# Gated delta rule with a gated convolution behind it: a third tap of the convolution as a diagonal product on TensorE, and a new order of all instructions

## The chip, the core and the metric

The kernel runs on one core of a Trainium2 chip. The engines are named as the profile names them: PE (TensorE, the matrix engine; PEld is its loading of weights), DVE (VectorE), ACT (ScalarE), POOL (GpSimd), and SP, which here only issues transfers (DMA). The metric is the device time of one execution in microseconds. Three runs of the kernel before took 335.29, 337.51 and 338.4 us, so its median is 337.51 us.

## The reference

Two stages follow each other. The first is a recurrent attention with the delta rule, for 4 batches and 8 heads, 768 tokens, head size 48:

```python
k_n = k / (norm(k) + 1e-6)
for t in range(S):
    y[:, :, t] = einsum('bhd,bhde->bhe', q[:, :, t], state)
    v_old      = einsum('bhde,bhd->bhe', state, kt)
    state     += bt * einsum('bhd,bhe->bhde', kt, vt - v_old)
```

The second takes the 8 heads of a token as one row x of 384 numbers, and has a causal convolution over time with 5 taps for each channel, a sigmoid gate, and two products with 384x384 matrices:

```python
gate_pre = sum(conv_w[k] * xp[:, k:k + S, :] for k in range(5))   # xp: x behind 4 rows of zeros
out = (sigmoid(gate_pre) * (x @ w_val)) @ w_out
```

All of it is in float32. The three weight arrays come to the kernel as the bits of float64 numbers, which it turns into float32 itself.

## The kernel before, in words

The 768 tokens are cut into 12 chunks of 64. Two chunks make a group, so there are 6 groups. All 32 pairs of batch and head are worked on at once; two heads share the 128 partitions, 16 such pairs lie side by side.

**Preparation of a group (`prep`).** For each half of a chunk a load brings keys and queries (`KQ`, three buffers, 448 KB each), and PE makes the products of all keys with all keys and queries (`gram`, 16 matmuls). ACT copies them out (`GL`) and gathers the diagonal blocks (`D`). DVE then inverts 32x32 triangular blocks: a transpose into `TLP`, the norms and coefficients (`coef`), rows and merges (`row`, `mergez8`, `zmul`, `tred` and so on, with some of the large products on POOL), and two transposes out, `TTR` and `TNA`. This is the longest stretch of work on DVE. PE combines the blocks with `z` and `t` (32 small matmuls each for a chunk), and ACT copies the results to `BD`.

**The chain of a chunk (`chain`).** `e` (keys on the state), `u` (the inverse on the values), `SPS` (the update of the state, kept in PSUM) and `y` (the output). Each step waits for a copy of the step before: `VT` on DVE, `US` on ACT. POOL scales the values (`vscale`) and masks the products of queries and keys (`att`, into `AQ`). The rows of `y` go to `X` by a copy on ACT and, where they change partitions, by six small transfers from `YS` for each chunk.

**The second stage of a chunk (`moe`).** For each of 3 blocks m of 128 channels: `conv`, the taps listed in `PTAPS`, as matmuls of 128x128 diagonal weights `DW` with 256 columns of `X` into a bank of PSUM; `tap`, the other taps, each one instruction on DVE that multiplies a shifted view of `X` by a column of weights and adds it to the same bank; `sig`, the sigmoid, on ACT; `val`, 3 matmuls of 256 columns; `gate` on DVE. Then two output blocks `out` of 3 matmuls with 384 columns each, copied by ACT and stored.

A float32 matmul counts as two instructions on PE in the profile, so a `conv` with two taps is x4 there, a `val` x6, an `out` x6, a `gram` x32.

**What sets the order.** Every step is recorded in a plan with a number, and the table `ORDER` lists these numbers in the order in which they are issued; each engine works through its own part of this list strictly in turn. A negative number -n in the table stands for n calls of `keep_warm`, a matmul of zeros (`SPS<-ZW`, 128x128) whose result nobody uses; it occupies PE only. Loads stand in the same table, and SP issues them in that order. A load waits in SP's queue until its buffer is free, and everything behind it waits with it.

The weights pass through two staging places in turn (`plan_weights`): a load, five steps on bits (one on ACT, four on DVE: L275, L277, L279, L282), a copy on ACT and two instructions on POOL. There are seven such passes: the taps, three for `w_val`, three for `w_out`. `tap_weights` makes `DW` out of the identity and the taps, one ACT instruction for each tap and block.

```python
PTAPS = (0, 1)                                   # taps that go to PE
for i, k in enumerate(PTAPS):                    # conv(m), L700
    PE.matmul(p, DW[:, m, i, :], x[:, m, :, k:k + C], start=(i == 0), stop=(i == len(PTAPS) - 1))
V.scalar_tensor_tensor(out=p, in0=x[:, m, :, k:k + C], scalar=CW[:, m, k:k + 1], in1=p,   # tap(m, k), L705
                       op0=ALU.mult, op1=ALU.add)
for k in (k for k in range(KS) if k not in PTAPS):
    add("DVE", 0.48, tap, (m, k), r=XT_ + [("Xh", c), "CW"], w=kp)
```

Of the kernel before, what the change touches and what calls it, by code (L numbers as in the profile page):

```python
# [26 lines left out]
PTAPS = (0, 1)  # L27
# [4 lines left out]
    -1, 8, 16, 65, 160, 9, 70, -1, 3, 1, 2, 7, 75, -1, 10, 11, 12, -1, 13, -2, 14, 17, 0, 4, 6, -1, 15, 24, 64, 18,  # L32
    19, 20, 21, 22, -8, 66, 67, -1, 23, 69, 68, -1, 71, 80, -1, 72, 106, 32, 76, -1, 73, 74, -2, 77, 163, 272, 161,
    267, 25, 85, 79, 78, -1, 26, 27, -2, 81, -4, 28, 29, 30, 31, 82, -3, 33, 83, 84, 268, -2, 86, 34, 35, 36, 269,
    -1, 37, 38, 87, 270, 39, -4, 273, 88, 89, 110, 215, 107, 48, 162, 311, 277, 282, 90, -1, 274, 91, 276, 275, 92,
    93, -1, 94, 95, 96, 97, 98, -1, 99, -1, 100, 101, 102, 103, 111, 104, -1, 278, 279, 281, 280, 49, 283, -3, 472,
    40, 105, 112, 113, 114, 115, 116, 284, -7, 117, 118, -1, 41, 119, 120, 121, 122, 123, 125, 124, 5, 126, -1, 127,
    50, -2, 128, 42, -4, 43, 129, 51, 130, 131, 132, -1, 133, -2, 134, 44, 135, -1, 136, 45, 137, 138, -1, 139, 271,
    -3, 285, 286, 46, 47, 108, 140, 287, 288, 52, 141, -50, 142, 473, 143, 474, 144, 289, 475, 146, 147, 368, 109,
    56, 477, 482, 148, 290, 291, 292, 293, 294, 295, 53, 296, 149, -1, 478, 150, 54, 55, 479, 297, 298, 57, 145,  # L40
    299, 300, 301, 302, 168, 303, 481, 169, 304, 305, 58, 306, 307, 314, 315, 59, 316, 151, 317, 60, 318, 152, 170,
    153, 319, 61, 320, 62, 321, 63, 175, 156, 171, 172, 480, 322, 173, 164, 167, 216, 176, 155, 174, 677, 487, 166,
    309, 157, 177, 158, 476, 154, 159, 323, 217, 324, 483, 484, 218, 178, 486, 488, 219, 325, 489, 485, 221, 328,
    329, 220, 330, 331, 222, 362, 513, 165, 363, 181, 184, 183, 180, 308, 182, 312, 179, 227, 310, 326, 327, 364,
    332, 490, 224, 223, 228, 369, 333, 334, 336, 370, 340, 337, 229, 230, 186, 193, 187, 188, 194, 189, 200, 231,
    233, 235, 234, 236, 232, 682, 190, 313, 335, 367, 237, 185, 195, 225, 201, 196, 202, 191, 226, 197, 338, 192,
    339, 203, 204, 198, 245, 341, 199, 205, 238, 252, 343, 246, 239, 492, -1, 491, 493, 206, 342, 211, 348, 212,
    207, -1, 344, 494, 208, 678, 345, 346, 247, 495, 240, 496, 248, 241, 497, 679, 681, 680, 498, -1, 499, -1, 500,
    -1, 683, 501, 253, 502, 684, -1, 356, 249, 503, 504, 254, 505, 506, 507, 508, 349, 686, 242, 685, 509, 510, 350,
    357, 351, 243, 255, 511, 512, 519, 520, 352, 256, 347, 521, 244, 522, 523, 250, 353, 354, 251, 524, 525, 526,  # L50
    257, 355, 358, 359, 371, 372, 258, 527, 420, 210, 213, 692, 209, 366, 687, 516, 365, 374, 528, 373, 529, 688,
    689, 380, 530, 375, 691, 360, 361, 376, 690, 381, 377, 693, 259, 573, 214, 887, 514, 533, 534, 260, 262, 261,
    531, 378, 694, 421, 535, 536, 422, 537, 382, 718, 892, 379, 695, 383, 532, 569, 389, 385, 386, 538, 423, 387,
    384, 388, 882, 424, 263, 426, 432, 539, 425, 541, 542, -1, 427, 543, 540, 391, 433, 696, 428, 429, 430, 545,
    544, 392, 393, 431, 264, 394, 515, 546, 398, 434, 395, 435, 396, 547, 574, 698, 697, 572, 390, 549, 517, 883,
    405, 550, 440, -1, 441, -1, 439, 438, 437, 436, 399, 397, 884, 548, 575, 699, -1, 457, 700, 458, 551, 553, 554,
    -1, 885, 886, 552, 562, 701, 459, 460, 555, 888, 889, 702, 406, 703, 461, 443, 407, 704, 400, 705, 890, 556,
    557, 891, 706, 444, 707, -1, 558, 559, -2, 893, 445, 708, 709, 446, 710, 711, -1, 894, 712, 401, 713, 568, 1087,
    897, 265, 266, 447, 408, 714, 715, 450, 716, 717, 451, 724, 402, 895, 896, 409, 403, 410, 576, 560, 725, 726,
    404, 727, 728, 411, 448, 563, 564, 416, 729, 452, 730, 453, 731, 449, 732, 733, 734, 412, 417, 561, 454, 565,  # L60
    566, 413, 419, 567, 418, 415, 625, 721, 414, 570, 735, 455, 462, 898, 577, 456, 518, 736, 737, 463, 578, 738,
    739, 899, 571, 1092, 579, 900, 585, 580, 586, 581, 582, 740, 468, 464, 719, 741, 742, 743, 583, 469, 465, 584,
    626, 746, 744, 587, 466, 1097, 923, 747, 627, 750, 628, 629, 588, 631, 901, 630, 748, -2, 632, 442, 745, 774,
    720, 590, 594, 637, -2, 633, 593, 778, 592, 589, 591, 722, 470, 830, 635, 634, 638, -1, 639, 749, 751, 902, 640,
    775, 646, 645, 643, 776, 773, 641, 642, 471, 644, 467, 772, 752, 753, 903, 610, 779, 595, 777, 723, 611, 780,
    904, 612, 754, 1088, 755, 756, 766, 767, 1089, 596, 603, 1102, 1091, 757, 1090, 905, 597, -1, 906, 613, -2,
    1093, 614, 1094, -1, 907, 598, 908, 909, 604, 910, 599, 911, 605, 912, 913, 606, -1, 662, 759, 760, 1096, 1095,
    914, 663, 915, 664, 916, 917, 665, 918, 600, 758, 636, 761, 763, 615, 762, 666, 607, 919, 920, 616, 648, 921,
    649, 922, 650, 929, 781, 1098, 667, 782, 930, 668, 931, 651, 932, 784, 652, 1099, 764, 783, 933, 934, 1101, 765,
    935, 785, 1103, 655, 787, 1104, 936, 937, 656, 938, 786, 831, 1100, 1105, 939, 788, 601, 602, 940, 657, 658,  # L70
    768, 769, 789, 770, 771, 659, 1106, 608, 790, 609, 832, 941, 942, -1, 653, 833, 660, 943, 834, 791, 792, 983,
    924, 654, 944, 661, 945, 946, 835, 947, 621, 836, 793, 948, 837, 617, 842, 798, 799, 1128, 797, 794, 796, 795,
    838, 618, 622, 843, 840, 844, 925, 979, 949, 800, 647, 841, 845, 801, 951, 952, 953, 955, 950, 624, 623, 851,
    927, 848, 619, 977, 620, 1035, 849, 847, 808, 802, 803, 815, 809, 804, 816, 810, 673, 811, 805, 839, 817, 954,
    818, 984, 806, 819, 674, 675, 676, 846, 978, 850, 928, 982, 956, 812, 1107, 807, 957, 820, 669, 813, 821, 985,
    958, 959, 960, 860, 867, 963, 1108, 961, 962, 670, 1109, 861, 1110, 814, 853, 964, 965, 826, 1111, 862, 868,
    869, 1112, 870, 1113, 863, 1114, 1115, 854, 966, 871, 972, 827, 872, 672, 671, 828, 1131, 829, 981, 1116, 864,
    855, 1117, 1118, 873, 1119, 1120, 856, 1121, 865, 1122, 1123, 967, 971, 857, 1124, 968, 1125, 1126, 969, 986,
# [758 lines left out]
```

## Time and profile before

| | |
|---|---|
| median of three runs | 337.51 us |
| the profiled execution, whole | 338.18 us |
| its span, first to last instruction | 336.5 us |
| PE busy with matmuls | 308.9 us (92%) |
| PE loading weights | 251.0 us (75%) |
| DVE busy | 261.8 us (78%) |
| ACT busy | 193.3 us (57%) |
| POOL busy | 124.7 us (37%) |

The profiled execution lies 0.67 us above the median, and 1.68 us of it lie outside the span. Two cautions: matmuls are pipelined and their ends are modelled, so PE's busy time also holds short gaps; and the granted clock of PE (PEclk, 1.00 is full speed) differs between stages. A row of a table by stages gives for one stretch of time the busy microseconds of each engine with the number of its instructions, then the mean granted clock, the mean busy share of the 16 DMA engines, and the GB/s that they moved. In a row of the timeline or the chain the first number is the start, the second the length, and what stands in brackets is the idle time of that engine just before and what ended it.

### The profile page before, as it was taken

How to read it: one execution, taken by the hardware profiler on the slowest of the kernel's cores; microseconds unless marked ns; L12 is line 12 of the kernel's file. 1: busy time of each engine (PE TensorE's matmuls, PEld its weight loads, DVE VectorE, ACT ScalarE, POOL GpSimd, SP SyncE). 2: the span in 40 equal slices, each digit the busy share in tenths (PEclk: the TensorE clock that was granted, in tenths of full speed). 3: DMA queues.
4: the chain of work that ended last, by engine and by line, in shares of the span. 5: the costliest groups of instructions: out<-in, count | busy, mean ns of one | idle time of the engine just before them, and what ended most of it. 6: DMA issues, size and time to landing. Idle time of an engine off the chain costs nothing.

```text
span 336.5 us, 13878 instructions
## 1 busy us (share of the span) xinstructions
PE 308.9 (92%) x6050; PEld 251.0 (75%) x6050; DVE 261.8 (78%) x565; ACT 193.3 (57%) x428; POOL 124.7 (37%) x92
## 2 busy tenths in 40 slices
PE   8936999699779979999999999999999999999994
PEld 6835899589757868777787887868776787786872
DVE  5368999999698994999997899896998779511640
ACT  6742402987636865598455897534875633575221
POOL 5441355244980005960057620485200583300000
PEclk9987599755997998999999999999999999999999
DMA  7899805045440573625087664014341742301222
GB/s 213 265 205 262 191 0 158 3 113 170 128 123 1 137 185 113 179 59 159 15 222 209 186 131 150 8 57 131 107 115 37 204 109 79 96 4 27 47 47 47
DMA packets 20283, 39.47 MB, mean 117 GB/s; under 512 B 8112, under 2 KB 11312, under 8 KB 20224
## 3 DMA queue, kind: packets, MB, share of 16 engines
q1 hardware_dynamic: 20224, 38.60, 43.5%
q8 instruction: 47, 0.77, 1.0%
q14 instruction: 12, 0.10, 0.1%
HBM read 32.69 MB, written 4.72 MB: 111 GB/s over the span
## 4 chain that ended last, share of the span: by engine, by line
PE 60%; DVE 14%; ACT 8%; DMA 7%; POOL 4%; issue 3%; SPq 3%; POOLq 0%; ACTq 0%; DVEq 0%
PE out L726 14%; PE val L715 11%; PE conv L700 7%; PE gram L358 4%; PE e L581 4%; PE u L581 3%; PE SPS L769 3%; PE y L649 3%; SPq L221 3%; PE SPS L581 2%; PE y L651 2%; PE z L458 2%; DMA AQ<-in_w_val_dram 2%; PE t L478 2%; DMA X<-YS 2%
## 5 line engine op out<-in xcount | busy, mean ns | idle before, releaser
L705 DVE SCALAR_TENSOR_TENSOR conv<-X,CW,conv 128x256 f32<-128x256 f32 x108 | 49.9, 484 | 14.2 <-PE conv L700 12.1
L715 PE MATMUL val<-X,WV 128*128 128x256 f32 x216 | 52.5, 390 | 0.0
L726 PE MATMUL out<-WO,GT 128*128 128x384 f32 x144 | 50.9, 495 | 0.0
L421 POOL TENSOR_TENSOR PR<-TLP,TT__83 128x768 f32<-128x768 f32 x5 | 10.6, 2118 | 97.0 <-DVE TT__83 L416 97.0
L715 PEld LDWEIGHTS val<-X,WV 128*128 128x128 f32 x216 | 40.3, 192 | 6.9 <-ACT GL L216 0.3
L769 PE MATMUL SPS<-ZW 128*128 128x128 f32 x294 | 43.7, 302 | 0.4 <-ACT US L643 0.4
L769 PEld LDWEIGHTS SPS<-ZW 128*128 128x128 f32 x294 | 39.4, 210 | 5.1 <-issue 3.6
L358 PE MATMUL gram<-KQ 48*64 48x128 f32 x768 | 33.4, 311 | 10.2 <-DMA KQ<-in_kq_dram 8.5
L700 PE MATMUL conv<-X,DW 128*128 128x256 f32 x144 | 37.5, 396 | 2.7 <-POOL X L695 2.3
L726 PEld LDWEIGHTS out<-WO,GT 128*128 128x128 f32 x144 | 26.2, 189 | 15.0 <-DVE GT L719 0.2
L216 ACT ACTIVATE GL<-gram 128x512 f32<-128x512 f32 x48 | 27.1, 596 | 16.7 <-PE gram L358 16.2
L358 PEld LDWEIGHTS gram<-KQ 48*64 48x64 f32 x768 | 26.1, 156 | 13.6 <-issue 9.3
L649 PE MATMUL y<-AQ,US 112*64 112x64 f32 x384 | 31.0, 237 | 4.7 <-issue 4.0
L649 PEld LDWEIGHTS y<-AQ,US 112*64 112x64 f32 x384 | 26.8, 147 | 8.9 <-issue 7.7
L700 PEld LDWEIGHTS conv<-X,DW 128*128 128x128 f32 x144 | 26.5, 194 | 8.4 <-POOL X L695 2.7
L559 POOL TENSOR_SCALAR_AFFINE_SELECT AQ<-GL 64x1024 f32<-64x1024 f32 x24 | 29.2, 1216 | 7.2 <-PE y L649 3.5
L216 ACT ACTIVATE D<-GL 32x512 f32<-32x512 f32 (+1 forms) x36 | 22.6, 628 | 15.8 <-DVE TT__83 L441 15.1
L581 PE MATMUL u<-VT,BD 64*64 64x48 f32 x768 | 30.6, 233 | 0.7 <-DVE VT L633 0.6
L581 PEld LDWEIGHTS u<-VT,BD 64*64 64x64 f32 x768 | 27.7, 148 | 3.8 <-issue 1.1
L651 PE MATMUL y<-AQ,US 128*48 128x64 f32 x384 | 29.1, 233 | 0.0
L633 DVE TENSOR_TENSOR VT<-e,VT 128x384 f32<-128x384 f32 x22 | 12.3, 557 | 20.1 <-PE e L581 14.1
L637 ACT ACTIVATE US<-u 64x384 f32<-64x384 f32 x24 | 11.6, 483 | 27.9 <-PE u L581 27.8
(97 smaller groups left out, 609.7 us busy)
## 6 DMA issues: line engine op xcount, KB each, us to landing
KQ<-in_kq_dram SPq DMA_DIRECT2D x24, 448.0 KB, 5.6
KF<-in_kf_dram SPq DMA_DIRECT2D x11, 448.0 KB, 4.6
KT<-in_kt_dram SPq DMA_DIRECT2D x12, 384.0 KB, 4.2
AQ<-in_qf_dram SPq DMA_DIRECT2D x24, 192.0 KB, 4.5
VT<-in_vt_dram SPq DMA_DIRECT2D x12, 384.0 KB, 4.0
out_dram<-OS SPq DMA_DIRECT2D x48, 96.0 KB, 2.7
AQ<-in_w_val_dram SPq DMA_DIRECT2D x3, 384.0 KB, 6.0
AQ<-in_w_out_dram SPq DMA_DIRECT2D x3, 384.0 KB, 7.6
```

The costliest lines, as they stand in the source:

```text
L216: A.activation(out=out, in_=in_, func=AF.Copy, **kw)
L358: PE.matmul(bank["g", g, c, 2 * h + s][64 * a:64 * a + 64, 128 * j:128 * (j + 1)], x[:, 0:C], x, start=True, stop=True)
L559: G.affine_select(out=AQ[c][r0:r0 + 64, j], in_=GL[r0:r0 + 64, c * NP:(c + 1) * NP, 64:128], pattern=[[0, NP], [1, C]], compare_op=ALU.is_ ...
L581: return lambda: PE.matmul(*a, stop=True, **k)
L633: V.tensor_tensor(out=v, in0=bank["e", ch, h][:, 0:HB * D].rearrange("p (u x) -> p u x", x=D), in1=v, op=ALU.add)
L649: PE.matmul(p[0:64, C * j:C * j + C], US[ch % 3][0:112, 0, h, D * j:D * j + 64], AQ[c][0:112, 0, pp, :], start=True, stop=True)
L651: PE.matmul(p[64:112, C * j:C * j + C], us[:, 1, h, j, :], AQ[c][:, 1, pp, :], start=True, stop=True)
L700: PE.matmul(p[:, 0:B * C].rearrange("p (b t) -> p b t", t=C), DW[:, m, i, :], x[:, m, :, k:k + C], start=(i == 0), stop=(i == len(PTAPS) - 1))
L705: V.scalar_tensor_tensor(out=p, in0=x[:, m, :, k:k + C], scalar=CW[:, m, k:k + 1], in1=p, op0=ALU.mult, op1=ALU.add)
L715: PE.matmul(p[:, 0:B * C].rearrange("p (b t) -> p b t", t=C), WV[:, k, 128 * m:128 * m + 128], xs[:, k], start=(k == 0), stop=(k == NKT - 1))
L726: PE.matmul(bank["o", ch, i][:, 0:DM], GT[k][:, 2 * i:2 * i + 2, :].rearrange("p b t -> p (b t)"), WO[:, k, :], start=(k == 0), stop=(k == ...
L769: PE.matmul(SPS[0][:, 384:512], ZW, ZW, start=False, stop=True, skip_group_check=True)
```

## The change

`PTAPS` becomes `(0, 1, 2)`. So each `conv` has three matmuls instead of two, `DW` holds nine diagonal blocks instead of six, and of the five taps two remain on DVE instead of three. Over 12 chunks and 3 blocks, 36 instructions leave DVE and 36 matmuls come to PE.

The numbers of the plan's steps shift with it, and the table `ORDER` is another one throughout: 1256 steps instead of 1292, and 172 calls of `keep_warm` instead of 147. Nothing else differs; line numbers are 3 lower after the table.

```diff
-PTAPS = (0, 1)
+PTAPS = (0, 1, 2)
...
 ORDER = [
-    -1, 8, 16, 65, 160, 9, 70, -1, 3, 1, 2, 7, 75, -1, 10, 11, 12, -1, 13, -2, 14, 17, 0, 4, 6, -1, 15, 24, 64, 18,
+    0, 8, 16, 160, 9, 65, 1, 10, 11, 12, 13, 70, 75, 14, 17, -1, 15, 6, 4, 64, 24, 18, 2, 19, 20, 21, -10, 66, 67,
...
```

Where the instructions stand, at three places. **First**, PE ahead of the first `z`, the first work that needs the inverse of group 0. Before (the second `gram` here is the eighth of the program):

```order
L358 MATMUL gram<-KQ_67 64x128 x16
L769 MATMUL SPS_120<-ZW 128x128 x3
L358 MATMUL gram<-KQ_68 64x128 x16
L769 MATMUL SPS_120<-ZW 128x128 x73
L458 MATMUL z<-TTR,GL_80 32x32 x32
L358 MATMUL gram<-KQ_69 64x128 x16
L478 MATMUL t_632<-ZS,TNA 32x32 x32
```

The same place now:

```order
L355 MATMUL gram<-KQ_67 64x128 x16
L766 MATMUL SPS_120<-ZW 128x128 x10
L355 MATMUL gram<-KQ_68 64x128 x16
L766 MATMUL SPS_120<-ZW 128x128 x107
L455 MATMUL z<-TTR,GL_80 32x32 x32
L766 MATMUL SPS_120<-ZW 128x128 x11
L355 MATMUL gram<-KQ_69 64x128 x16
L766 MATMUL SPS_120<-ZW 128x128 x2
L475 MATMUL t_701<-ZS,TNA 32x32 x32
```

Between the eighth `gram` and `z` stand 107 matmuls of zeros instead of 73. **Second**, SP's loads at the same time. Before (the first row is the 20th load of the program, the second brings the keys for the eighth `gram`):

```order
L221 DMA KQ_67<-in_kq_dram 112x1024
L221 DMA KQ_68<-in_kq_dram 112x1024
L221 DMA KQ_69<-in_kq_dram 112x1024
L221 DMA AQ_79<-in_w_out_dram 128x768
L221 DMA KF_76<-in_kf_dram 112x1024
L221 DMA KT_71<-in_kt_dram 128x768
L221 DMA AQ_79<-in_w_out_dram 128x768
```

Now, again from the 20th load on (here the load of `KQ_68` is the one for the eighth `gram`; `KQ_67` for the seventh was the 14th load):

```order
L218 DMA AQ_79<-in_w_out_dram 128x768
L218 DMA VT_75<-in_vt_dram 128x768
L218 DMA KT_72<-in_kt_dram 128x768
L218 DMA KQ_69<-in_kq_dram 112x1024
L218 DMA AQ_78<-in_qf_dram 48x1024
L218 DMA KQ_68<-in_kq_dram 112x1024
L218 DMA AQ_79<-in_w_out_dram 128x768
```

The keys for the eighth `gram` went from the 21st place to the 25th. Both lists of the first 25 loads hold the same things, but for one load of `KT` (384 KB) in place of one of `KF` (448 KB); the 26th is in both the last part of `w_out`. **Third**, PE around the first `z` of group 1 (`GL_81`). Before:

```order
L700 MATMUL conv<-X_98,DW 128x256 x6
L581 MATMUL SPS_121<-US_94,KT_71 48x48 x16
L715 MATMUL val<-X_98,WV 128x256 x6
L700 MATMUL conv<-X_99,DW 128x256 x2
L715 MATMUL val<-X_98,WV 128x256 x3
L700 MATMUL conv<-X_99,DW 128x256 x4
L769 MATMUL SPS_120<-ZW 128x128
L726 MATMUL out<-WO,GT_101 128x384 x6
L769 MATMUL SPS_120<-ZW 128x128
L458 MATMUL z<-TTR,GL_81 32x32 x32
L358 MATMUL gram<-KQ_67 64x128 x16
```

Now:

```order
L697 MATMUL conv<-X_98,DW 128x256 x6
L455 MATMUL z<-TTR,GL_81 32x32 x32
L697 MATMUL conv<-X_98,DW 128x256 x3
L712 MATMUL val<-X_98,WV 128x256 x3
L697 MATMUL conv<-X_99,DW 128x256 x3
L355 MATMUL gram<-KQ_67 64x128 x16
L712 MATMUL val<-X_98,WV 128x256 x3
L697 MATMUL conv<-X_99,DW 128x256 x3
L355 MATMUL gram<-KQ_68 64x128 x16
L475 MATMUL t_1406<-ZS,TNA 32x32 x32
L712 MATMUL val<-X_98,WV 128x256 x3
```

The `z` of group 1 stands ahead of most of the second stage of chunks 0 and 1 now, behind it before. Counted on PE's whole list from this `z` to the end: `conv` 60 matmuls before and 102 now, `val` 99 and 108, `out` 66 and 72, `keep_warm` 25 and 0, everything else the same. Between the first `z` of the program and this one: `conv` 12 and 6, `val` 9 and 0, `out` 6 and 0, `keep_warm` 3 and 16, the rest the same.

On DVE, ahead of `TTR` of group 0, twelve steps on the bits of `w_out` stand now where six stood; ahead of `TTR` of group 1, 11 taps (9 of chunk 0, 2 of chunk 1), 3 gates and `TNA` stood before, and none of them now.

121 rows, old and new, of the table ORDER are left out of this document.

## The prediction

> **What bounds the kernel now.** I read the table by stages first: where is PE full, and at which clock?
>
> ```profile
> core 0: us, PE busy (x) PEld busy (x) DVE busy (x) ACT busy (x) POOL busy (x), PEclk, DMA share, GB/s
> 30.00:40.00 10.00, 6.97 (x81) 5.93 (x81) 9.30 (x25) 3.06 (x6) 1.17 (x1) 0.65 1.02 238
> 40.00:50.00 10.00, 10.00 (x78) 10.00 (x78) 9.86 (x13) 2.01 (x5) 6.40 (x3) 0.84 0.04 13
> 50.00:58.00 8.00, 7.83 (x71) 7.64 (x69) 7.90 (x8) 1.67 (x3) 4.86 (x4) 1.00 0.57 166
> 58.00:64.00 6.00, 3.31 (x164) 2.65 (x164) 5.79 (x12) 5.78 (x13) 0.00 (x0) 0.97 0.02 4
> 64.00:70.00 6.00, 5.28 (x154) 5.01 (x156) 5.52 (x22) 4.36 (x10) 2.00 (x2) 0.50 0.41 115
> 70.00:84.00 14.00, 13.59 (x348) 12.84 (x346) 13.04 (x26) 11.76 (x26) 7.56 (x6) 0.50 0.41 120
> 84.00:91.00 7.00, 5.28 (x188) 4.96 (x180) 5.56 (x7) 3.88 (x9) 6.85 (x5) 0.99 0.61 155
> 91.00:100.00 9.00, 6.71 (x62) 5.32 (x59) 7.82 (x15) 3.85 (x8) 8.68 (x7) 1.00 0.33 94
> 110.00:135.00 25.00, 23.02 (x693) 19.05 (x693) 19.69 (x61) 17.49 (x42) 5.00 (x3) 0.93 0.58 149
> 159.00:246.00 87.00, 86.06 (x1836) 68.27 (x1836) 76.65 (x162) 55.73 (x127) 36.61 (x24) 1.00 0.45 118
> 284.00:332.00 48.00, 47.06 (x789) 35.64 (x774) 19.36 (x41) 22.44 (x56) 5.26 (x7) 1.00 0.17 39
> ```
>
> To 58 us DVE is full and PE mostly runs zeros; from 64 to 84 PE is busy at half clock; from 110 on it is full at full clock. Then the timeline of PE, for the marks between these stages:
>
> ```profile
> 37.61 1.99 PE L358 MATMUL gram<-KQ 48*64 48x128 f32 x32
> 39.53 18.30 PE L769 MATMUL SPS<-ZW 128*128 128x128 f32 x146
> 58.50 0.74 PE L458 MATMUL z<-TTR,GL 32*32 32x32 f32 x64 [0.67 <-DVE TTR L446]
> 91.07 2.87 PE L700 MATMUL conv<-X,DW 128*128 128x256 f32 x12
> 99.86 1.13 PE L700 MATMUL conv<-X,DW 128*128 128x256 f32 x4 [2.29 <-POOL X L695]
> 109.95 0.75 PE L458 MATMUL z<-TTR,GL 32*32 32x32 f32 x64
> ```
>
> The first z comes at 58.50, when DVE's TTR is ready; the z of group 1 at 109.95. That a busy PE is the bound and doesn't hide waits of its own is told by who waits for whom between 100 and 332 us (total, times, longest):
>
> ```profile
> PE u L581 <- DVE VT L633: 0.6, 1, 0.6
> PE z L458 <- DVE TTR L446: 0.6, 1, 0.6
> ...
> DVE VT L633 <- PE e L581: 13.6, 4, 6.6
> DVE conv L705 <- PE conv L700: 12.1, 5, 3.7
> DVE GT L719 <- PE val L715: 9.2, 11, 2.2
> DVE VT L633 <- PE u L581: 5.4, 3, 4.0
> ```
>
> DVE waits 40.3 us for PE there, PE 1.2 us for DVE. The chain of waits has the undisturbed prices, and the end:
>
> ```profile
> 159.20 4.07 PE val L715 x18
> 163.95 4.07 PE out L726 x12
> 198.23 0.87 PE conv L700 x4
> 332.17 0.49 ACT OS L216
> ```
>
> A conv of two matmuls takes 0.87 us, 0.435 each (256 columns). A val matmul has the same form: 18 instructions are 9 matmuls, 0.45 each. An out matmul is 4.07 / 6 = 0.68. PE ends at 332.17; the last copy and store end the span at 336.5, 4.3 later, and 1.7 us lie outside it.
>
> **The taps.** Groups of instructions:
>
> ```profile
> L705 DVE SCALAR_TENSOR_TENSOR conv<-X,CW,conv 128x256 f32<-128x256 f32 x108 | 49.9, 484 | 14.2 <-PE conv L700 12.1 <-ACT GT L709 0.7 <-DMA out_dram<-OS 0.3
> L769 PE MATMUL SPS<-ZW 128*128 128x128 f32 x294 | 43.7, 302 | 0.4 <-ACT US L643 0.4
> L700 PE MATMUL conv<-X,DW 128*128 128x256 f32 x144 | 37.5, 396 | 2.7 <-POOL X L695 2.3 <-DMA X<-YS 0.2
> L279 DVE SCALAR_TENSOR_TENSOR X<-AQ,X 128x384 uint32<-128x384 uint32 (+1 forms) x4 | 4.1, 1017 | 0.1
> L216 ACT ACTIVATE DW<-EYE,CW 128x128 f32<-128x128 f32 x6 | 1.9, 390 | 0.2 <-POOL CW L290 0.2
> ```
>
> DVE loses 36 of 108 taps, 49.9 / 3 = 16.6 us; nearly all lie where it waits for PE, so their removal alone gains about nothing. PE gets 36 matmuls: 36 x 0.435 = 15.7 us, or by the group's busy time 37.5 / 2 = 18.8. Both ends lie on the bound; I take 0.435, measured in a full queue. The added product also stands before sig instead of a tap of 0.484, so a PSUM bank is held as long as before. ACT makes three more blocks of DW, 3 x 0.31 = 0.9 us in the first 8 us, hidden by the loads that the first transpose waits for; uncovered it would be 0.9.
>
> **The start.** Here the order decides. The DMA engines are full until 40 us (share 1.02, then 0.04): the first 25 loads are through by then, and SP stands still. The changed list loads nearly the same 25 things first, but the keys for the eighth gram are the 25th instead of the 21st. So that gram begins at about 40.5 instead of 37.61 and ends at 42.5. Behind it stand 107 keep_warm, 214 instructions. Before, 146 took 18.30 us from a low clock; 68 more at 7.83 / 71 = 0.110 us add 7.5: the zeros end at 68.3. TTR was ready just before 58.50; six more bit steps on DVE, at the dearest mean (L279, 1.017), bring it to 64.5 at most, and the 26th load, for which the last of them wait, lands about 42, before DVE gets there. So the zeros hold z, at about **68.4**, 9.9 us later than before (bounds 65.5, if all 214 go at 0.110 from 42, and 70).
>
> From the first z to the z of group 1 took 51.4 us. At that pace the changed list takes less: 6 conv (2.6), 9 val (4.1) and 6 out (4.1) have gone behind, 13 keep_warm (26 x 0.110 = 2.9) were added: 43.5, so 111.9. The other end is no wait at all at full clock. The stage lost up to 10 us by half a clock over 20 us, 2.7 idle at 58 to 64, and 4.0 idle at 84 to 100 (1.7 + 2.3): 16.7 in all, so 95.2. I take **100**, nearer to that end: PE comes into z warm from the zeros, all that z, t and u need from DVE is ready, and the copy on POOL for which conv waited 2.29 stands ahead of the masks now. But t and u still wait for ACT's copies, and four of the six small transfers into X stand on SP behind a load of values that waits for u of chunk 1.
>
> ```profile
> 101.05 1.95 DVE L448 STREAM_TRANSPOSE TNA<-TT__83 128x1024 f32<-128x1024 f32 x1
> 105.28 0.42 DVE L719 TENSOR_TENSOR GT<-val,GT 128x256 f32<-128x256 f32 x1
> 105.61 2.04 DVE L446 STREAM_TRANSPOSE TTR<-TT__83 128x1024 f32<-128x1024 f32 x1
> ```
>
> DVE agrees: its TTR of group 1 ended at 107.65; away from ahead of it go 11 taps (11 x 0.484 = 5.3), 3 gates (1.3) and TNA (2.0), which leaves 99.
>
> The Trainium skill (TensorE: Matmul & The Clock Gate, Part 1: The HAM clock gate) says that PE's clock is halved by default, released by about 3.4 us of sustained work, and halved again after an idle window of that length; by it the clock would hold from 68 to 100, and the sum is the 100 that I take. This trace bears it out only in part: from 70 to 84 the clock was 0.50 with PE busy 13.59 of 14.00; if that comes back, the sum is the first rival's.
>
> **From there to the end.** Before: 332.17 - 109.95 = 222.2 us. Added: 42 conv (18.3), 9 val (4.07), 6 out (4.07) = 26.4. Gone: 25 keep_warm, 50 of 294 instructions, between 50 x 0.110 = 5.5 and 43.7 x 50 / 294 = 7.4; I take 6.5. At 110 to 135 PE lost 2.0 idle and 1.7 by clock (0.93); with DVE relieved I take half of it back, 1.9 (bounds 0 and 3.7). 222.2 + 26.4 - 6.5 - 1.9 = 240.2. PE ends at 100 + 240.2 = 340.2, the span at 344.5, and with 1.7 outside it an execution like the profiled one takes 346.2, 8.0 over its 338.18. That one stood 0.7 above the median, so I forecast **345.5 us** against 337.51.
>
> **Rivals.** *Slow start.* The small matmuls between z and conv run at half clock again, as from 64 to 84; only the rearranged work goes: z of group 1 at 107 to 112, end 7 to 12 us later, 352.5 to 357.5. For it: the clock stayed at 0.50 for 20 us though PE was busy. Against: it fell after the idle pieces from 58 to 64, and 13 zeros more stand there now. Chance 0.18.
>
> *All slack is taken back.* z of group 1 at 95.2, keep_warm worth 7.4, the 3.7 saved: 345.5 - 4.8 - 0.9 - 1.8 = 338.0, no change. For it: PE's queue has no zeros left behind group 1, so it seems to have work at hand everywhere. Against: u, e and y still wait for copies. With the middle between it and the forecast, chance 0.24.
>
> *PE is not full, and DVE set the pace (faster).* In the row 159 to 246 PE loads weights for 68.27 of 87 us, 78%, and DVE is busy 76.65, 88%. If the matmuls only look dense because they wait in the array, a third of a conv slips into the gaps; with all 18.3 us hidden the stage to the end takes 222.2 + 8.1 - 6.5 = 223.8, and the time is 100 + 223.8 + 4.3 + 1.7 - 0.7 = 329.1; with half of it hidden, 338. It makes the kernel faster from 13 hidden us on (334.1). Against it: DVE's 40.3 us of waiting for PE, and 9 val in 4.07 us, as dense as the 0.435 of conv. Chance 0.14. The Trainium skill (Perfetto Trace Analysis, Identifying the Most-Contended Engine) speaks for this one: it calls matmul busy time a bad measure and wants the share of weight loading; by that PE has 22% left, and the time would be the 329.1. The waits of this trace speak against it.
>
> My forecast, 340.9 to 351, has the remaining 0.44.
>
> **How the numbers follow.** A change under 1%, 334.1 to 340.9, counts as none, since three runs spread over 335.29 to 338.4. Faster comes from the third rival alone: 0.13. Same from the second, with the rest of the third: 0.25. Slower from forecast and first rival: 0.62. The range takes in the second rival and the near half of the first: 334 to 355, which leaves about a tenth on either side.
>
> **What would show it.** Right: zeros on PE without a break to about 68, z right behind them with no wait for TTR; PE's clock near 1.00 from 70 on; z of group 1 near 100; conv x216 with about 0.435 for a matmul; DVE's waits for PE grown above 40 us; no SPS<-ZW after group 1. Wrong: z at 60, which would mean that the 25th load came much earlier; or PE idle for DVE in the middle of the program; or a last stage shorter than 230 us.

## The result, and the profile after

The changed kernel takes **351.2 us** (median of four executions, 348.91 to 353.06) against 337.95 us for the kernel before, run beside it. It is slower by 13.3 us; the forecast was 8.0. The ratio on record is 1.045, 95% interval 1.040 to 1.051, while the quotient of the two medians is 1.039. Medians are taken over all executions and ratios over the undisturbed ones, and in what follows the two differ by up to 0.9%. The direction and the range of 334 to 355 held; the size did not, and 351.2 lies 0.2 us above the bounds of the forecast itself (340.9 to 351).

The profiled execution is the longest of the four: 353.06 us, span 351.3. Its table by stages, to be read like the one of before:

```profile
50.00:60.00 10.00, 10.00 (x92) 10.00 (x91) 9.83 (x8) 3.29 (x5) 9.77 (x6) 1.00 0.01 2
60.00:70.00 10.00, 10.00 (x148) 9.84 (x148) 9.11 (x30) 2.85 (x7) 1.73 (x2) 1.00 0.01 2
70.00:84.00 14.00, 11.20 (x338) 9.56 (x338) 7.80 (x19) 9.21 (x20) 4.67 (x2) 0.85 0.23 62
84.00:91.00 7.00, 6.90 (x241) 6.38 (x238) 2.46 (x4) 5.44 (x13) 1.48 (x1) 0.81 0.74 202
91.00:100.00 9.00, 7.21 (x221) 6.57 (x213) 6.79 (x8) 4.68 (x11) 4.20 (x2) 0.81 0.53 155
110.00:135.00 25.00, 24.82 (x581) 19.54 (x583) 22.06 (x69) 17.99 (x44) 5.18 (x4) 1.00 0.26 64
159.00:246.00 87.00, 83.46 (x1842) 67.40 (x1843) 70.47 (x147) 53.41 (x121) 33.80 (x22) 0.96 0.44 119
284.00:332.00 48.00, 47.05 (x890) 37.39 (x889) 17.57 (x30) 23.09 (x57) 5.09 (x6) 1.00 0.29 71
332.00:347.00 15.00, 14.96 (x58) 10.52 (x56) 4.02 (x9) 2.51 (x6) 0.00 (x0) 1.00 0.12 26
```

PE is full from 110 on, nearly as before (from 159 to 246 it works 83.46 us at a clock of 0.96, where it was 86.06 at 1.00). It is full from 50 to 70 too, but with zeros. From 70 to 100 it stands still for 4.7 us, runs at 0.81 to 0.85, and DVE, which worked 13.04 of the 14 us from 70 to 84 before, now works 7.80. The marks on PE's timeline:

```profile
42.02 25.91 PE L766 MATMUL SPS<-ZW 128*128 128x128 f32 x214
67.86 0.75 PE L455 MATMUL z<-TTR,GL 32*32 32x32 f32 x64
79.05 0.99 PE L578 MATMUL u<-VT,BD 64*64 64x48 f32 x26 [2.50 <-ACT ZS L213]
103.30 2.84 PE L697 MATMUL conv<-X,DW 128*128 128x256 f32 x12 [1.56 <-DMA X<-YS]
106.07 0.80 PE L455 MATMUL z<-TTR,GL 32*32 32x32 f32 x64
```

The 107 zeros run without a break to the first `z`, which waits for nothing else: `TTR` of group 0 had ended at 59.87, so the data of `z` were ready 8.0 us before. Between `z` and `u` 11.2 us pass. On DVE the first step of the state chain in this stretch waits 10.19 us for `e`, and DVE has nothing else to do meanwhile:

```profile
88.47 0.56 DVE L630 TENSOR_TENSOR VT<-e,VT 128x384 f32<-128x384 f32 x1 [10.19 <-PE e L578]
93.18 0.56 DVE L630 TENSOR_TENSOR VT<-e,VT 128x384 f32<-128x384 f32 x1 [2.07 <-PE e L578]
103.44 2.15 DVE L443 STREAM_TRANSPOSE TTR<-TT__83 128x1024 f32<-128x1024 f32 x1
```

Groups of instructions, then the chain's undisturbed prices and its end:

```profile
L697 PE MATMUL conv<-X,DW 128*128 128x256 f32 x216 | 53.2, 390 | 4.4 <-DMA X<-YS 3.4 <-issue 0.9
L702 DVE SCALAR_TENSOR_TENSOR conv<-X,CW,conv 128x256 f32<-128x256 f32 x72 | 34.7, 488 | 27.5 <-PE conv L697 24.8 <-ACT D L213 0.9 <-issue 0.6
```

```profile
251.96 4.10 PE conv L697 x18
347.05 0.49 ACT OS L213
```

Nine matmuls of `conv` take 4.10 us, 0.456 each; the group grew by 53.2 - 37.5 = 15.7 us for 36 matmuls. DVE's taps fell from 49.9 to 34.7.

The span splits at the two marks of the prediction. All numbers are from the profiled executions:

| stretch | before | forecast | after |
|---|---|---|---|
| start to the first `z` | 58.50 | 68.4 | 67.86 |
| first `z` to `z` of group 1 | 51.45 | 31.6 | 38.21 |
| `z` of group 1 to the end of PE | 222.2 | 240.2 | 240.98 |
| end of PE | 332.17 | 340.2 | 347.05 |

One row is wrong, by 6.6 us, and that is nearly all of the 6.85 us between forecast and trace. Two more marks split this row: the first `u`, and the first `conv`, which is chunk 0's. Before, `conv` stands at 91.07 and `u` at 66.48:

```profile
66.48 1.91 PE L581 MATMUL u<-VT,BD 64*64 64x48 f32 x32
```

| part of the row | before | after |
|---|---|---|
| first `z` to first `u` | 7.98 | 11.19 |
| first `u` to first `conv` | 24.59 | 24.25 |
| first `conv` to `z` of group 1 | 18.88 | 2.77 |

All that the new order gains here lies behind the first `conv`. Up to it chunk 0's chain takes 35.4 us instead of 32.6.

### The profile page after: what moved, and what is told of

The parts are those of the page before. It is cut to its first block, busy times and chain, and to the rows that moved or that the text cites. A ratio compares the mean times of both kernels' runs of the same rounds, so it can differ in the third digit from the quotient of the medians.

```text
span 351.3 us, 14079 instructions
## 1 busy us (share of the span) xinstructions
PE 321.5 (92%) x6172; PEld 263.1 (75%) x6172; DVE 251.0 (71%) x529; ACT 193.5 (55%) x431; POOL 124.9 (36%) x92
## 4 chain that ended last, share of the span: by engine, by line
PE 76%; DMA 10%; ACT 8%; DVE 2%; issue 2%; SPq 1%; ACTq 0%; DVEq 0%
PE val L712 14%; PE out L723 13%; PE conv L697 13%; PE SPS L766 8%; PE e L578 6%; PE gram L355 4%; DMA KQ<-in_kq_dram 4%; PE u L578 4%; PE y L646 3%; PE y L648 3%; PE SPS L578 3%; DMA KT<-in_kt_dram 3%; PE z L455 2%; PE t L475 2%; DMA AQ<-in_w_val_dram 2%
## 5 line engine op out<-in xcount | busy, mean ns | idle before, releaser
L697 PE MATMUL conv<-X,DW 128*128 128x256 f32 x216 | 53.2, 390 | 4.4 <-DMA X<-YS 3.4
L702 DVE SCALAR_TENSOR_TENSOR conv<-X,CW,conv 128x256 f32<-128x256 f32 x72 | 34.7, 488 | 27.5 <-PE conv L697 24.8
L697 PEld LDWEIGHTS conv<-X,DW 128*128 128x128 f32 x216 | 40.0, 190 | 12.8 <-issue 3.7
L766 PEld LDWEIGHTS SPS<-ZW 128*128 128x128 f32 x344 | 42.3, 202 | 3.4 <-issue 3.2
L418 POOL TENSOR_TENSOR D<-TLP,TT__83 128x1024 f32<-128x1024 f32 x6 | 16.0, 2660 | 65.3 <-DVE TT__83 L413 65.3
L578 PEld LDWEIGHTS u<-VT,BD 64*64 64x64 f32 x768 | 26.4, 142 | 6.9 <-issue 5.5
L556 POOL TENSOR_SCALAR_AFFINE_SELECT AQ<-GL 64x1024 f32<-64x1024 f32 x24 | 27.5, 1145 | 6.3 <-PE y L646 5.4
L578 PE MATMUL e<-US,KF 48*64 48x48 f32 x704 | 25.9, 220 | 3.5 <-issue 3.0
L646 PE MATMUL y<-AQ,US 112*64 112x64 f32 x384 | 29.0, 231 | 0.0
L578 PEld LDWEIGHTS e<-US,KF 48*64 48x64 f32 x704 | 22.7, 134 | 5.4 <-issue 2.6
```

The source lines that it names most:

```text
L418: eng.tensor_tensor(out=buf[:, 0:64 * n].rearrange("p (k i j) -> p k i j", k=4, i=16), op=ALU.mult, in0=tl4[:, 1, :, 0, 4 * kb:16].unsquee ...
L556: G.affine_select(out=AQ[c][r0:r0 + 64, j], in_=GL[r0:r0 + 64, c * NP:(c + 1) * NP, 64:128], pattern=[[0, NP], [1, C]], compare_op=ALU.is_ ...
L578: return lambda: PE.matmul(*a, stop=True, **k)
L646: PE.matmul(p[0:64, C * j:C * j + C], US[ch % 3][0:112, 0, h, D * j:D * j + 64], AQ[c][0:112, 0, pp, :], start=True, stop=True)
L697: PE.matmul(p[:, 0:B * C].rearrange("p (b t) -> p b t", t=C), DW[:, m, i, :], x[:, m, :, k:k + C], start=(i == 0), stop=(i == len(PTAPS) - 1))
L766: PE.matmul(SPS[0][:, 384:512], ZW, ZW, start=False, stop=True, skip_group_check=True)
```

## The experiments

Fifteen kernels. The time is the median in us; the kernel before ran beside each group of runs (medians of 335.7 to 337.0), and the ratio on record is to that.

| kernel | time (range) | ratio, 95% interval |
|---|---|---|
| `tap_old_order` | 351.82 (350.55 to 356.02) | 1.043, 1.037 to 1.050 |
| `new_order_old_tap` | 348.38 (343.74 to 349.31) | 1.030, 1.020 to 1.039 |
| `zero_tap_on_pe` | 353.04 (350.04 to 355.5) | 1.045, 1.037 to 1.053 |
| `one_tap_less` | 335.95 (333.94 to 344.03) | 0.998, 0.994 to 1.003 |
| `after_73_zeros` | 339.5 (338.11 to 342.03) | 1.014, 1.005 to 1.022 |
| `after_fill_before_u` | 353.45 (347.54 to 356.16) | 1.059, 1.050 to 1.069 |
| `after_e_late` | 350.84 (349.43 to 353.96) | 1.048, 1.039 to 1.058 |
| `one_tap_on_pe` | 347.22 (342.69 to 348.98) | 1.028, 1.015 to 1.042 |
| `after73_late_dve` | 337.95 (332.66 to 342.49) | none: the four times lie too far apart |
| `after73_old_tap` | 339.22 (338.9 to 341.75) | 1.014, 1.006 to 1.022 |
| `before_84_zeros` | 344.1 (338.64 to 346.99) | 1.015, 1.002 to 1.027 |
| `before_zeros_behind_z` | 345.95 (341.62 to 350.7) | 1.028, 1.016 to 1.039 |
| `after_short_chain` | 346.16 (344.39 to 350.0) | 1.031, 1.023 to 1.039 |
| `after73_short_chain` | 338.38 (336.87 to 344.94) | 1.007, 1.003 to 1.011 |
| `after73_short_late` | 335.01 (332.57 to 338.66) | 0.992, 0.988 to 0.996 |

### The tap and the order, each alone

`tap_old_order` gives the tap to PE and keeps the order of before:

```diff
-PTAPS = (0, 1)
+PTAPS = (0, 1, 2)
...
     def tap(m, k):
+        if k in PTAPS:
+            return
```

> The third tap goes to PE, and the order of before is kept: the steps of 36 taps on DVE are empty, everything else stands where it stood. Theory A (PE is full behind the z of group 1, a product of 256 columns costs it 0.435 us, and DVE's relief is worth little): 337.95 + 36 x 0.435 = 353.6, at least 350 us. Rival B (the new order, with its 107 matmuls of zeros ahead of z and SP held behind them, costs most of the 13 us, and the tap alone is hidden): at most 343 us.

`new_order_old_tap` takes the order of after, with the third tap on DVE:

```diff
-PTAPS = (0, 1, 2)
+PTAPS = (0, 1)
...
+    def taps(m, k):
+        if k == 3:
+            tap(m, 2)
+        tap(m, k)
```

> The order of the changed kernel, but the third tap is an instruction on DVE again, issued just ahead of the fourth tap; 36 products leave PE. Theory A: 351.2 - 15.7 = 335.5, between 333 and 339 us, about the kernel before. Rival B: 346 us or more, for the order itself is what is slow.

The tap alone costs as much as the whole change, 351.82 us, as theory A had it. The order alone costs 3.0%, which theory A had not expected and theory B had. The two costs don't add up: 4.3% and 3.0% together give 4.5%. So within the new order the tap costs little (2.8 us by the medians), and what the new order costs has to be found.

### PE's share and DVE's share of the tap

`zero_tap_on_pe` is the kernel before with one more matmul of zero weights in each `conv`; DVE keeps its three taps. `one_tap_less` is the kernel before without the third tap; the convolution lacks one of its five taps there.

```diff
+            PE.matmul(p, ZW, x[:, m, :, 2:2 + C], start=False, stop=True)    # zero_tap_on_pe
```

```diff
     def tap(m, k):
+        if k == 2:
+            return                                                          # one_tap_less
```

> The kernel before with a third product in each conv whose weights are zeros; DVE still does all of its three taps. So PE's load grows as in the change, and DVE's stays. Theory A: 353 us, within 1% of the run with the tap moved in the old order; DVE's 36 instructions are worth under 2 us. Rival (the taps taken from DVE do give something back): 3 us or more above that run.

> The kernel before without the third tap: neither PE nor DVE does it, so the convolution lacks one of its five taps; DVE has 36 instructions (16.6 us) less, PE the same work. Theory A: 336 to 338 us, no change. Rival C (DVE sets the pace with PE): 328 us or less.

Both came out as theory A said. The matmuls of zeros, in the groups of `zero_tap_on_pe`:

```profile
L702 PE MATMUL conv<-X,ZW 128*128 128x256 f32 x72 | 21.5, 378 | 0.0
```

Work added to PE alone makes the kernel before 4.5% slower; the same work with DVE's relief makes it 4.3% slower; the relief alone brings nothing that can be measured. In the order of before PE sets the pace and DVE's third tap was free.

`one_tap_on_pe` goes the other way from before: one tap on PE, four on DVE.

```diff
-PTAPS = (0, 1)
+PTAPS = (0,)
```

> The kernel before with one tap of the convolution as a product instead of two, and three on DVE: 36 products fewer than before (15.7 us of PE), 36 more instructions on DVE (about 17.4 us). Theory A (PE is full and sets the pace; the tap that went to PE cost 15.9 us in the order of before): 320 to 326 us. Rival D (DVE, with 279 us of work, then holds PE up): no gain, 333 to 345 us.

Theory A fails here: 347.22 us, slower than before. The interval of the ratio allows 5 to 14 us, so rival D's range (333 to 345) is not excluded. Taking 36 matmuls off PE gains nothing if DVE gets the work. In the order of before the split of before, two and three (336 us), has a slower neighbour on both sides (351.8 and 347.2).

### How many zeros ahead of the first z

`after_73_zeros` is the kernel after with before's number of zeros at that place:

```diff
-    ..., 281, 282, -96, 142, 461, 143, -11,
+    ..., 281, 282, -62, 142, 461, 143, -11,
```

> The kernel after with 73 zeros instead of 107 ahead of the first z. In its trace the 107 zeros took 25.91 us, 0.242 each, so 34 fewer end 8.2 us sooner, at 59.6, about when DVE hands over the first transposed block; z at about 60. Theory S (the late start of group 1 is DVE's: its row work for group 1 stands behind steps that wait for the products e, which follow the first z; the longest wait was 10.19 us): e comes some 8 us sooner, DVE's wait shrinks to about 2 us, z of group 1 comes at 98 and the end 241 us behind it: 343 us, 340 to 346. Rival K (the clock): with fewer zeros the clock falls to half from about 64 on, as before, and the products between z and e take back what was won: z of group 1 at 104 to 106, 349 us or more.

339.5 us: of the 13.3 us, 11.7 are back. From the timeline of PE:

```profile
60.43 0.74 PE L455 MATMUL z<-TTR,GL 32*32 32x32 f32 x64 [0.60 <-DVE TTR L443]
69.68 0.96 PE L578 MATMUL u<-VT,BD 64*64 64x48 f32 x26 [0.57 <-ACT BD L464]
92.15 5.03 PE L697 MATMUL conv<-X,DW 128*128 128x256 f32 x12 [2.00 <-DMA X<-YS]
97.10 0.75 PE L455 MATMUL z<-TTR,GL 32*32 32x32 f32 x64
```

`z` comes 7.4 us sooner and now waits 0.60 us for `TTR`: so the other 34 zeros held back a `z` whose data were ready. `z` of group 1 comes 9.0 us sooner, 36.7 behind `z`. The time lies just below theory S's range. Its mechanism is not what this trace shows: DVE's `TTR` of group 1 ended at 94.05, 3.0 us ahead of `z` of group 1. What stands right ahead of that `z` is chunk 0's first `conv`, which waited for the transfer into `X`.

`before_84_zeros` does the reverse to the kernel before:

```diff
-    ..., 141, -50, 142, 473, 143,
+    ..., 141, -84, 142, 473, 143,
```

> The kernel before with 34 more zeros ahead of the first z, 8.2 us by 0.242 each. Theory Z (the first z sets the time, in this order too): z at 66.7 instead of 58.5 and 344 us (342 to 346). Rival D (in the order of before group 1's start hangs on DVE's taps and its transposed block, not on the first z): less than half of that, 340 us or less.

The median rose by 8.1 us, as theory Z had it, but the four times reach from 338.64 to 346.99, and the ratio's interval allows 1 to 9 us. In the profiled execution `z` came at 63.9 (5.4 later) and the span was 340.0 (3.5 longer). The direction is shown, one for one is not.

### Is it the clock?

`after_fill_before_u` puts 18 more zeros into the pause ahead of the first `u`:

```diff
-    308, 471, 168, 309,
+    308, 471, -18, 168, 309,
```

> The kernel after with 18 more zeros in the 2.5 us in which PE stood still ahead of the first u (76.5 to 79.05); at full clock they take about that long. Rival K: the clock doesn't fall to 0.64, 0.50 and 0.72 behind it, the products up to e take some 3 us less, z of group 1 comes at 103 and the time is 348 us (347 to 349.5). Theory S without a share of the clock: e is delayed or as it was, z of group 1 at 106 or later, 351 us or more.

Two rows of its table by stages, and lines of its timelines of PE and ACT:

```profile
79.00:82.00 3.00, 3.00 (x124) 2.67 (x128) 0.00 (x0) 1.88 (x4) 2.88 (x2) 1.00 0.03 5
82.00:85.00 3.00, 2.00 (x110) 1.71 (x102) 0.00 (x0) 2.85 (x7) 0.00 (x0) 1.00 0.82 240
```

```profile
65.00 0.75 PE L453 MATMUL z<-TTR,GL 32*32 32x32 f32 x64
74.50 1.52 ACT L211 ACTIVATE ZS<-z 32x256 f32<-32x256 f32 x4
74.68 4.29 PE L764 MATMUL SPS<-ZW 128*128 128x128 f32 x36 [0.98 <-issue]
78.89 0.96 PE L576 MATMUL u<-VT,BD 64*64 64x48 f32 x26
102.13 2.84 PE L695 MATMUL conv<-X,DW 128*128 128x256 f32 x12 [1.45 <-DMA X<-YS]
104.90 0.75 PE L453 MATMUL z<-TTR,GL 32*32 32x32 f32 x64
```

The same two slices in the kernel after:

```profile
79.00:82.00 3.00, 2.95 (x64) 2.68 (x64) 0.00 (x0) 0.97 (x2) 3.00 (x2) 0.64 0.03 5
82.00:85.00 3.00, 3.00 (x102) 2.69 (x104) 0.00 (x0) 1.69 (x3) 0.30 (x1) 0.50 0.52 158
```

The zeros held the clock at 1.00 there, but they did not fit into the pause. They took 4.29 us, not 2.5; the 0.242 for one that the expectation of `after_73_zeros` had worked out gives 4.4 for 18. ACT's copies, for which `u` had waited, had ended at 76.02, and `u` came at 78.89. So `u` follows `z` by 13.9 us instead of 11.2, and `conv` follows `u` by 23.2 instead of 24.3: the zeros cost 2.7 us, and the part behind them, at the higher clock, gave 1.0 back. The five times reach from 347.54 to 356.16 us, and no gain shows. This run can't take the clock out of the account, because its zeros delayed the chain that they were to speed up.

A cleaner pair is `after_73_zeros` and `after73_old_tap` (below). They issue the same instructions from `z` to the first `conv`, and from 70 to 84 the one ran at full clock, the other at about half:

```profile
70.00:84.00 14.00, 11.70 (x472) 10.23 (x470) 12.89 (x28) 11.23 (x27) 5.91 (x3) 1.00 0.58 171
```

```profile
70.00:84.00 14.00, 14.00 (x371) 12.78 (x370) 10.21 (x23) 8.75 (x21) 6.29 (x3) 0.55 0.48 138
```

From `u` to `conv` they took 22.5 and 25.7 us. At 0.55 some 6 us of PE's work are lost in 14 us, and 3.2 show. The kernel after took 24.3 for this part, so its slow stretches cost it some 1.8 us there (an estimate, against the 22.5 at full clock), of the 6.6 to be explained. Rival K names a part of the cause and not most of it.

`before_zeros_behind_z` tries the same in the order of before, with 12 zeros behind the first `z`:

```diff
-    142, 473, 143, 474, 144, 289, 475, 146, 147, 368,
+    142, 473, 143, -11, 474, 144, 289, 475, 146, -1, 147, 368,
```

> The kernel before with 12 zeros behind the first z, at the places where the order of after has them. In the trace of before the clock was 0.71 and 0.50 from 59 to 84; with 73 zeros in the order of after it was 1.00 there. Rival K (the slow clock costs before some 5 us): 328 to 332 us. Theory Z (the chain from z to u, e and y goes through ACT and DVE and isn't shortened by the clock): 334 to 338 us, or slower by the zeros' 2.9 us.

345.95 us, 10 us slower than before; rival K had expected a gain, and theory Z at most 338 or 2.9 us for the zeros. Why 12 zeros cost more than their own length wasn't settled.

### Is it DVE's wait for e?

`after_e_late` lets DVE do eight steps of group 1's rows ahead of the steps that wait for `e`, and PE the `z` of group 1 ahead of chunk 0's first `conv`:

```diff
-    ... 214, 323, 324, 325, ... 217, 326, 327, 330, ... 331, 332, 333, ... 186, ... 198, 338, 339,
+    ... 323, 324, 325, 326, 327, 214, ... 330, 331, 332, 217, ... 333, ... 338, 339, 186, ... 198,
```

> The kernel after with two changes of order: on DVE five steps of group 1's row work go ahead of the first step that waits for e (it waited 10.19 us), and three more ahead of the second; on PE z of group 1 goes ahead of chunk 0's first convolutions, which waited 1.56 us for their data. Theory S: DVE fills its wait with that work, z of group 1 comes at 97 to 100, and the end follows 241 us behind it: 344 us, 341 to 347. Rival Y (the end follows chunk 0's own chain, z, u, e, y, convolution, and not z of group 1): z of group 1 comes earlier, but the end doesn't move by more than 2 us: 349 us or more.

DVE's wait shrank as meant, from 10.19 to 3.43 us, but a later one grew from 2.07 to 5.18. The third line is PE's:

```profile
88.38 0.56 DVE L628 TENSOR_TENSOR VT<-e,VT 128x384 f32<-128x384 f32 x1 [3.43 <-PE e L576]
98.83 0.56 DVE L628 TENSOR_TENSOR VT<-e,VT 128x384 f32<-128x384 f32 x1 [5.18 <-PE e L576]
103.61 0.83 PE L453 MATMUL z<-TTR,GL 32*32 32x32 f32 x64 [3.83 <-DVE TTR L441]
```

`TTR` ended at 103.55 instead of 105.59, and `z` of group 1, now waiting for it, came at 103.61 instead of 106.07, short of the 97 to 100 expected. The first `conv`, which had stood ahead of this `z`, now starts behind it, at 104.37 instead of 103.30. The time stayed at 350.84. Rival Y's number holds; theory S's does not, but DVE gave back only 2.0 us here, so what an earlier `TTR` would be worth is not shown. In the kernel after, `TTR` ends 0.5 us ahead of `z` of group 1 and the `conv` just as it starts, so shortening either alone can gain little.

### Is it the chain of chunk 0?

`after_short_chain` leaves out the 11 zeros between the first `z` and the next `gram`, and puts the first `u` ahead of the second `z`, with its copies on ACT. `after73_short_chain` does it with 73 zeros.

```diff
-    142, 461, 143, -11, 462, ... 469, 145, ... 151, 152, ... 168, ... 153, 169,
+    142, 461, 143, 462, ... 145, 469, ... 168, 151, 152, ... 169, 153,
```

> The kernel after (107 zeros) with the links between the first z and the first u shortened: the 11 zeros between the first z and the gram are left out (2.7 us ahead of t), the first u goes ahead of the second z on PE, and its copies go ahead on ACT (u waited 2.5 us there for the copies of the second z). Theory Y (from z to z of group 1 it is chunk 0's own chain, each link waiting for the one before): z of group 1 comes some 4 us sooner, at 101 to 103, and the time is 347 us (345 to 348.5). Rival P (the stretch is set by something else, the clock or all of PE's work): 350 us or more.

> The same with 73 zeros ahead of the first z (339.5 us). Theory Y: z of group 1 at 92 to 94 instead of 97.1 and 335.5 us (334 to 337). Rival P: 339 us or more.

From the timeline of PE in `after_short_chain`:

```profile
64.94 0.75 PE L453 MATMUL z<-TTR,GL 32*32 32x32 f32 x64
71.58 1.14 PE L576 MATMUL u<-VT,BD 64*64 64x48 f32 x32 [1.19 <-ACT BD L462]
96.31 4.52 PE L695 MATMUL conv<-X,DW 128*128 128x256 f32 x12 [2.88 <-DMA X<-YS]
100.75 0.75 PE L453 MATMUL z<-TTR,GL 32*32 32x32 f32 x64
```

346.16 us, 5.0 less than after, as theory Y had it. `u` follows `z` by 6.6 us instead of 11.2, and the first `conv` follows `z` by 31.4 instead of 35.4: nearly all of the shortened link arrives. `z` of group 1 follows by 35.8 instead of 38.2, only 2.4 less, because from 97 to 100 the clock was at 0.50 and the six matmuls of `conv` took 4.52 us instead of 2.84. Another 2.9 us come from `z` itself, at 64.94 instead of 67.86 though nothing changed ahead of it, and that is not due to the edit (it was 65.00 in `after_fill_before_u` too). With 73 zeros the gain was 1.1 us, 339.5 to 338.38, between theory and rival. There `u` came 1.8 us sooner behind `z`, but the clock was 0.50 from 70 to 79 where `after_73_zeros` had 1.00, and `conv` came 3.3 us later behind `u`.

| kernel | `z` to `u` | `u` to `conv` | `conv` to `z` of group 1 |
|---|---|---|---|
| after | 11.19 | 24.25 | 2.77 |
| `after_fill_before_u` | 13.89 | 23.24 | 2.77 |
| `after_73_zeros` | 9.25 | 22.47 | 4.95 |
| `after73_old_tap` | 9.25 | 25.71 | 3.68 |
| `after_short_chain` | 6.64 | 24.73 | 4.44 |
| `after73_short_chain` | 7.48 | 25.79 | 2.78 |

In all six `z` of group 1 follows at once behind this `conv`, and the `conv` had waited for the transfer into `X`. So chunk 0's chain, which goes through PE, ACT, DVE and the transfers, sets this stretch, with `TTR` close to it in the kernel after. In eight profiled executions with the new order and chunk 0's three taps on PE the stretch took 35.8 to 39.9 us. In the kernel after 7.6 of the 24.25 us between `u` and `conv` lie behind SP's first transfer into `X`, issued at 95.69; what sets the rest, apart from the clock, was not settled.

### What the tap costs in an order that starts in time

`after73_old_tap` is `after_73_zeros` with the third tap on DVE; `after73_late_dve` has it on DVE in the last four chunks only.

```diff
+            n = 3 if ch < 8 else 2                  # after73_late_dve; the tap itself goes to DVE there
-            for i, k in enumerate(PTAPS):
+            for i, k in enumerate(PTAPS[:n]):
```

> The order of after with 73 zeros, and the third tap on DVE everywhere. Tells what the tap costs in an order that starts in time. If PE sets the pace throughout, 36 products fewer than the 339.5 us: 324 us (322 to 327). If the gain is lost again to waits for DVE, as with 107 zeros (348.4 against 351.2 us): 336 to 340 us.

> The kernel after with 73 zeros ahead of the first z (339.5 us), and its third tap back on DVE in the last four chunks alone: 24 products fewer (10.4 us of PE by 0.435 each), 24 instructions of 0.49 us more on DVE. With 73 zeros PE was busy for 85.0 of the 86 us from 246 to 332 and DVE for 42.7. Theory A (PE is full there and sets the pace, DVE has room): 329 to 332 us. Rival D (the instruction on DVE stands between product and sigmoid, and PE waits for what follows): 336 us or more.

`after73_old_tap` takes 339.22 us, `after_73_zeros` 339.5: here the tap costs nothing. The busy times, of `after_73_zeros` and then of `after73_old_tap`:

```profile
PE 314.3 (92%) x6104; PEld 255.5 (75%) x6104; DVE 248.9 (73%) x529; ACT 193.7 (57%) x431; POOL 124.1 (36%) x92
```

```profile
sum 355.00, PE 303.10 PEld 244.19 DVE 267.25 ACT 193.18 POOL 124.71; mean PE 25.26 PEld 20.35 DVE 22.27 ACT 16.10 POOL 10.39
```

With the tap on DVE PE has 11.2 us less to do and stands still for 36.9 us of a span of 340.0 instead of 26.0 of 340.3. This order is laid out for three taps on PE; with the third on DVE it stalls. What the tap costs is a property of the order: 15.9 us in that of before, about nothing here.

`after73_late_dve` came out at 337.95 us with a spread of 10 us, which decides nothing by itself. `after73_short_late` joins it with the shorter chain:

> The same with 73 zeros and with the third tap on DVE in the last four chunks (without the shorter links 337.95 us). Theory Y: 334 us (332 to 336), level with the kernel before. Rival P: 337 us or more.

335.01 us over 12 executions against 336.95 for the kernel before: 0.6% by the medians, 0.8% by the ratio (interval 0.4 to 1.2%), and some 5% below the kernel after (0.992 / 1.045 = 0.949). Its expected bounds held. It has three PE taps in eight chunks and two in four, 73 zeros, and the shorter links. The interval excludes that there is no gain over before, but a gain of this size counts as the same time (under 1%, as in the prediction).

## Why the prediction was right or wrong

- **Zeros to 68.3, z at 68.4.** Right: 67.86, and no wait for `TTR`. That the zeros cost time is shown: 34 fewer give back 11.7 us. The agreement to 0.5 us has luck in it, for in other executions of the same list `z` came at 65.00 and 64.94.
- **z of group 1 at 100.** This is the step that failed: the term "first `z` to `z` of group 1, 31.6 us" measured 38.2. The prediction took before's 51.4, moved 7.9 us of work away, and took back 11.9 of 16.7 us of lost time, up to 10 of them for the half clock; 4.8 us of lost time were left. In the trace PE stood idle for 6.26 us of the stretch, hardly less than the 7.33 of before, and the mean clock of 0.87 is worth some 5.0 us more (an estimate, 0.13 x 38.2): 11.3 in place of 4.8.

```profile
58.50:109.95 51.45, 44.12 (x924) 37.94 (x924) 45.61 (x87) 34.83 (x72) 25.09 (x18) 0.77 0.32 88
67.86:106.07 38.21, 31.95 (x909) 28.33 (x908) 24.12 (x45) 24.35 (x55) 14.88 (x8) 0.87 0.46 129
```

  The path was wrong, too: the term adds up PE's work, but the stretch is as long as chunk 0's chain up to its first `conv`, behind which the new order puts `z` of group 1. That mark stood in the prediction's lines, 91.07 - 58.50 = 32.57 us behind `z`, and all the work that was moved away stood behind it. With the prediction's own prices, in a sum made afterwards, it gives 68.4 + 32.57 + 2.6 (6 `conv`) + 2.9 (added zeros) = 106.5; it was 106.07. A full clock shortens the chain by little: even with the 22.5 us from `u` to `conv` of `after_73_zeros` the stretch of after would be 36.4 (an estimate: 11.2 + 22.5 + 2.8). The higher end, 43.5, was nearer than the value taken.
- **DVE agrees, 99.** Wrong: `TTR` ended at 105.59. The working took away what was moved out from ahead of it and left out that DVE's own steps wait for `e`, which comes behind a `z` that was just found to be 9.9 us later. In the kernel before that step ran at 77.71, now at 88.47. The check used the old start for a shifted chain, and so confirmed a number that it should have contradicted.
- **From z of group 1 to the end, 240.2.** Right as a sum: 241.0. PE's busy time in this part grew by 18.4 us where the terms have 26.4 - 6.5 = 19.9, and its idle time grew by 0.4, from 5.55 to 5.91, where the terms take 1.9 back for idle time and clock. That the two errors nearly cancel is luck. The group of `conv` grew by 15.7 us, exactly 36 x 0.435, though the undisturbed row prices one at 0.456.

```profile
109.95:332.17 222.22, 216.67 (x4629) 170.52 (x4628) 171.68 (x388) 134.61 (x312) 73.50 (x49) 0.99 0.41 107
106.07:347.05 240.98, 235.07 (x4693) 185.96 (x4692) 170.44 (x367) 140.27 (x323) 76.76 (x53) 0.99 0.36 95
```

- **DVE's taps gain about nothing.** Right in the order of before (ratio 0.998, 0.994 to 1.003).
- **Signs.** No zeros behind group 1, right: the last `SPS<-ZW` runs at 83. DVE's waits for PE above 40 us, right; between 100 and 340 us:

```profile
DVE conv L702 <- PE conv L697: 24.8, 17, 5.3
DVE GT L716 <- PE val L712: 12.3, 15, 2.1
DVE VT L630 <- PE e L578: 9.4, 4, 5.0
DVE VT L630 <- PE u L578: 7.0, 7, 2.3
```

  That is 53.5 us. PE, for its part, waits 3.4 us for transfers into `X` there, and none of its listed waits is for DVE. PE's clock near 1.00 from 70 on was wrong: 0.85, 0.81 and 0.81 up to 100.
- **The rivals.** *Slow start* came nearest in size (`z` of group 1 at 107 to 112; it was 106.07), but the clock that it blames accounts for some 1.8 of the 6.6 us up to `conv`. *All slack taken back* is out. *PE is not full* is out for the order of before: work added to PE alone cost 4.5%. The Trainium skill (Perfetto Trace Analysis, Identifying the Most-Contended Engine) would have had room for these matmuls by the share of weight loading (75% of the span before); `zero_tap_on_pe` decides against that reading here, as the waits had done.
- **What the forecast never asked** is whether the new order is good for its own start. It took 107 zeros as given and priced them rightly, but only the runs showed that the order without 34 of them loses 1.4% in place of 4.5%.

## What to carry to other kernels

Filler ahead of the first dependent step costs in full from the moment the step's data are ready, so compare those two times whenever an order is redrawn. When a start is forecast to shift, shift every chain that hangs on it before using another engine's timeline as a second opinion. Where PE, ACT, DVE and transfers wait for each other in turn, measure the chain from mark to mark in the trace of before; neither work moved away from behind its last mark nor the whole of a faster clock comes off it. What it costs to move an instruction between engines holds for one order only: add it, remove it, and move it in both orders before calling an engine the bound.

## What was not expected of the hardware

The same list of instructions did not start at the same time in each execution. Ahead of the first `z` nothing differs between the kernel after, `after_fill_before_u` and `after_short_chain`, but `z` came at 67.86, 65.00 and 64.94. About 2 of the 2.9 us come from a load: the eighth `gram` waited for its keys till 40.11 in the first, and till 38.13 and 37.88 in the others. The rest comes from the 107 zeros, which took 25.91, 25.02 and 25.21 us; from 40 to 50 the granted clock was 0.71, 0.91 and 0.90. The `gram` in the kernel after, then `gram` and zeros in `after_fill_before_u`:

```profile
40.11 1.98 PE L355 MATMUL gram<-KQ 48*64 48x128 f32 x32 [8.50 <-DMA KQ<-in_kq_dram]
```

```profile
38.13 1.98 PE L353 MATMUL gram<-KQ 48*64 48x128 f32 x32 [5.44 <-DMA KQ<-in_kq_dram]
40.05 25.02 PE L764 MATMUL SPS<-ZW 128*128 128x128 f32 x214
```

From 70 to 84 two kernels with the same instructions up to the first `conv` had a granted clock of 1.00 and 0.55. In the kernel after a pause of 2.5 us of PE (76.5 to 79.05) was followed by 0.64 and 0.50. The Trainium skill (TensorE: Matmul & The Clock Gate, Part 1: The HAM clock gate) puts the idle window at about 3.4 us; here the clock fell behind a shorter pause.
